# Weights decoded to half their value with a sign from ScalarE, and two heads gathered by matmul

## The chip, the cores and the metric

The kernel runs on one core of a Trainium2 chip. The metric is the device time of one execution in microseconds, median of the runs shown.

## The reference

Two stages follow each other: a linear attention with complex decay, and a feed-forward block. In short:

```python
# q, k, v, a_re, a_im: (4, 8, 768, 48); w_in (384, 2048), w_out (2048, 384)
mag = sqrt(a_re**2 + a_im**2); scale = minimum(mag, 0.999) / (mag + 1e-6)
a = (a_re + 1j * a_im) * scale
for t in range(768):                       # state S: (4, 8, 48, 48), complex
    S = a[:, :, t, :, None] * S + k[:, :, t, :, None] * v[:, :, t, None, :]
    y[:, :, t] = einsum("bhd,bhde->bhe", q[:, :, t], S.real)
x = y as (3072, 384)
h = x @ w_in;  g = h * sigmoid(1.702 * h);  out = g @ w_out
```

w_in and w_out are in double precision (the random factor times a float64 scalar), so the kernel is handed 64-bit words and makes single-precision numbers of them itself.

## The kernel before

**Tiling.** The 3072 tokens are 12 units of 256 (`T`). Unit 0 is prepared in two halves of 128 (`L`), the other units whole. Units form seven groups (`GROUPS`): unit 0, unit 1, then pairs. For each unit three things happen. `prepare` turns a_re, a_im, q and k into scaled and rotated q and k: squares, logarithms and exponentials on ScalarE, backward and forward products as scans on VectorE (`scan_sp`, L358, and `scan_qm`, L378), a running angle (L398), sine and cosine on ScalarE, then two rotations on VectorE (`rot0` into tile qr, `rot1` into tile qk). `remap` (L452 to L456) moves the rotated rows by DMA from a layout with 128 rows to one with 96 rows per head (tile qkh). `attend` computes scores, keys, outputs and state by small matmuls on TensorE. `moe` multiplies a group's outputs with w_in (`hidden`, L657), applies Silu on ScalarE, and multiplies with w_out (`project`, L686).

**Weights.** Eight blocks A0 to A7 of w_in and eight, U0 to U7, of w_out, each 128 x 768 64-bit words. `convert` decodes a block: a DMA loads it into one of four raw buffers; L249 shifts the top word left by three and masks it, L252 ORs in bits 31 and 30 of the top word, L255 (ScalarE) shifts the low word right by 29 in place, L256 adds. An integer add of tensors on VectorE runs as a custom operation on 16-bit halves. Group 0 uses the decoded single-precision values (`x`, `valA`, `valU`). From group 1 on each product is three products of rounded parts: `split` makes a high part by a ScalarE copy (L269) and a low part by a VectorE subtraction (L274); the matmuls then read `hiA`, `loA`, `xhi`, `xlo`.

**Checks of the input.** `inspect` and `angles` look over the data on VectorE; a slow general version stands behind a branch at the end and is not taken with this data.

**Order.** All operations are put into a plan with names of what they read and write, and issued in the order that the list `ORDER` (L1004) spells out. Each engine and the DMA queue of SyncE (SP) is in order, so `ORDER` sets each engine's queue. The durations in `add(...)` are the planner's; they set nothing at run time. ScalarE's table loads (L890) are put in where an operation's `tab` differs from the last one. Before the first scores there are 20 discarded matmuls against an identity (`WARM`, L434), 15 of them ahead of the first score matmul; they read the second rotation's tile.

**Set-up on POOL.** POOL makes the identity, the mask (12 small copies, L160), clears the two state tiles (L163), and then writes edge values (L338, L342, L392) that the scans read.

Of the kernel before, what the change touches and what calls it, by code (L numbers as in the profile page):

```python
# [8 lines left out]

# [4 lines left out]
U8 = mybir.dt.uint8  # L14
BF16 = mybir.dt.bfloat16
# [36 lines left out]
W_MIN = 2.0**-15  # L52
# [37 lines left out]
WARM = 20  # L90
# [5 lines left out]
def attention_moe(ctx: ExitStack, tc: tile.TileContext, qk_in, v, a_in, w_in, w_out, qn, kn, vn, an, bn, out):  # L96
# [65 lines left out]
    for x in st:  # L162
        nc.gpsimd.memset(x, 0.0)  # L163

# [19 lines left out]
    def d_t(n, fast=1.0):  # L184
        return 0.07 + n * 0.00104 / fast
# [47 lines left out]
    def convert(n):  # L233
# [6 lines left out]
        ulow = words.bitcast(U32)[:, :, 0]  # L240
        kg, kl = f"g{n % RAWS}", f"gl{n % RAWS}"
        rk = conv_rank(n)

        def ti():
            return weights.whole(m, j).bitcast(I32)
# [4 lines left out]
            out=ti(), in0=top, scalar1=3, scalar2=0x3FFFFFFF, op0=ALU.logical_shift_left, op1=ALU.bitwise_and,  # L250
        ), r=[kg], w=[f"v{c}"])
        add("DVE", d_t(WC), rk - 1, lambda: dve.scalar_tensor_tensor(  # L252
            out=ti(), in0=top, scalar=-(1 << 30), in1=ti(), op0=ALU.bitwise_and, op1=ALU.bitwise_or,
        ), r=[kg], w=[f"v{c}"])
        add("ACT", a_t(WC) - 0.1, rk - 1, lambda: act(out=low, in_=ulow, func=AF.Copy, scale=2.0**-29), w=[kl])  # L255
        add("DVE", d_t(WC), rk - 0.5, lambda: dve.tensor_tensor(out=ti(), in0=ti(), in1=low, op=ALU.add), r=[kl], w=[f"v{c}"])  # L256
# [41 lines left out]
    def prepare_part(u, i, a, b, np_, mag, den, rec, sp, th, *keys):  # L298
# [129 lines left out]
        for x, (dst, kd, fac, kf) in enumerate(((rv, "qr", cs, k_cs), (qv, "qk", t, k_th))):  # L428
# [3 lines left out]
            if u == i == 0 and x == 1:  # L432
                for k in range(WARM):
                    add("PE", 0.43, -WARM + k, lambda k=k, dst=dst: mm(  # L434
                        h_ps[0][:, k % 2 * T : (k % 2 + 1) * T], lhsT=ident, rhs=dst[:, k % NR, 0:T], start=True, stop=True
                    ), r=["qk0.0", "qk1.0"], w=["h0"])
# [3 lines left out]
            for some in ((0,), (1,)) if u == 0 else ((0, 1),):  # L440
                add("SP", REMAP * nn / (2 * T) * len(some) / 2, rk(f"rot{x}"), lambda dst=dst, x=x, some=some: remap(u, x, o, nn, dst, some),
                    r=ks(f"{kd}0", f"{kd}1") + ([f"last{x}"] if b == T else []), w=[f"H{hb_(u)}.{s}.{x}.{y}" for s in sub for y in some],
                    name=f"remap{u}.{i}.{x}" + ".1" * (some == (1,)), work=5)

# [180 lines left out]
    def moe(g):  # L625
# [7 lines left out]
        for order_, (lo, hi, f0) in enumerate(steps_):  # L633
# [30 lines left out]
            if whole:  # L664
                add("ACT", a_t(CW) - 0.15, rk(order_), lambda hb=hb, gb=gb: act(
                    out=high.g0(gb), in_=h_ps[hb], func=AF.Silu, scale=SLOPE
                ), r=[f"h{hb}"], w=[f"gh{gb}"], tab=SILU, name=f"G{u}.{order_}")
            else:
                add("ACT", a_t(CW) - 0.13, rk(order_), lambda hb=hb, gb=gb: act(out=high.g(gb), in_=h_ps[hb], func=AF.Silu, scale=SLOPE),  # L669
                    r=[f"h{hb}"], w=[f"gh{gb}"], tab=SILU, name=f"G{u}.{order_}")  # L670
                add("ACT", a_t(CW) - 0.13, rk(order_), lambda hb=hb: act(out=h_ps[hb], in_=h_ps[hb], func=AF.Silu, scale=SLOPE),  # L671
# [29 lines left out]
        for c in range(NR):  # L701
            buf, key = (osb[c], f"osb{c}")
            add("DVE", d_t(n_t), rk(len(steps_) + 0.1), lambda c=c, buf=buf: dve.tensor_scalar(
                out=buf[:, 0:n_t], in0=o_ps[c][:, 0:n_t], scalar1=1.0 / SLOPE, scalar2=None, op0=ALU.mult
# [442 lines left out]
```

## Time and profile before

| | us |
|---|---|
| median of 2 runs (552.05 to 552.52) | 552.28 |
| the profiled execution | 552.84 |
| its span, first to last instruction | 551.1 |
| TensorE matmul busy | 522.0 (95%) |
| VectorE busy | 390.0 (71%) |
| ScalarE busy | 362.2 (66%) |
| POOL busy | 11.9 (2%) |
| ScalarE table loads, 52 | 66.7 |

Engines in the profile: PE is TensorE's matmul, PEld its weight load, DVE is VectorE, ACT is ScalarE, SPq the DMA queue of SyncE. A single-precision matmul is two instructions in the trace. Busy shares are averages over stages that differ: the rows further down are cut by stage. Of a group of instructions, the mean is the duration of one; in a full queue the next one starts a little before the last one ends, so that the distance of two starts is shorter than the mean.

### The profile page before, as it was taken

To read this page: it belongs to the slowest core of one execution; us is meant where nothing else is said; L and a number is where in the kernel's file an instruction comes from. 1 tells how busy PE (TensorE), PEld (TensorE's weight loads), DVE (VectorE), ACT (ScalarE), POOL (GpSimd) and SP (SyncE) were. 2 spreads that over 40 slices of the span, in tenths; PEclk is the share of its full clock that TensorE was granted. 3 is DMA by queue.
4 is the path that set the end of the run, shared out by engine and by line. 5 is a ranking of instruction groups with operands and counts; after the bars stand their busy time and mean duration, and the time that the engine had idled before them with its cause. 6 is when DMAs were issued, how large, how long until landed. Compare 5 with 4: busy or idle time off the path is not lost.

```text
span 551.1 us, 14342 instructions
## 1 busy us (share of the span) xinstructions
PE 522.0 (95%) x6122; PEld 447.1 (81%) x6122; DVE 390.0 (71%) x625; ACT 362.2 (66%) x555; POOL 11.9 (2%) x55
## 2 busy tenths in 40 slices
PE   0399999999999999999999999999999999999997
PEld 0289988999988888888888888888888888888885
DVE  7999999999978787697598876785375524432232
ACT  7897899989699957968959578676425132232231
POOL 6000000000000000000000000000000000000000
PEclk9999999999999999999999999999999999999999
DMA  8867881835574764636548756518322552003101
GB/s 338 289 209 288 214 336 43 218 105 133 201 177 135 170 216 95 177 117 143 178 135 198 226 148 180 161 62 198 94 66 78 149 112 79 19 29 104 47 23 61
DMA packets 29253, 82.02 MB, mean 149 GB/s; under 512 B 4096, under 2 KB 7168, under 8 KB 29184
## 3 DMA queue, kind: packets, MB, share of 16 engines
q1 hardware_dynamic: 29184, 81.06, 50.6%
q8 instruction: 49, 0.80, 0.6%
q14 instruction: 20, 0.16, 0.1%
HBM read 57.41 MB, written 4.72 MB: 113 GB/s over the span
## 4 chain that ended last, share of the span: by engine, by line
PE 52%; ACT 2%; DVE 1%; issue 0%
PE o_ps L686 22%; PE h_ps L657 21%; PE x_ps L507 3%; PE z_ps L561 1%; PE z_ps L517 1%; PE p_ps L517 1%; PE p_ps L536 1%; PE z_ps L536 1%; ACT L890 0%; DVE qr L231 0%; ACT gh L669 0%; ACT h_ps L671 0%; ACT s L331 0%; ACT s L333 0%; ACT s L335 0%
## 5 line engine op out<-in xcount | busy, mean ns | idle before, releaser
L669 ACT ACTIVATE gh<-h_ps 128x512 fp32r<-128x512 f32 x88 | 52.1, 596 | 117.9 <-PE h_ps L657 92.2
L657 PE MATMUL h_ps<-xhi,hiA 128*128 128x512 f32 (+1 forms) x288 | 109.2, 379 | 0.0
L657 PE MATMUL h_ps<-xhi,loA 128*128 128x512 f32 (+1 forms) x288 | 107.1, 372 | 0.0
L657 PE MATMUL h_ps<-xlo,hiA 128*128 128x512 f32 (+1 forms) x288 | 107.1, 372 | 0.0
L673 DVE TENSOR_TENSOR gl<-h_ps,gh 128x512 fp32r<-128x512 f32 x88 | 60.0, 684 | 64.5 <-ACT h_ps L671 62.2
L686 PE MATMUL o_ps<-gh,hiU 128*128 128x512 f32 (+1 forms) x288 | 79.4, 376 | 0.2 <-ACT gh L669 0.2
L686 PE MATMUL o_ps<-gl,hiU 128*128 128x512 f32 (+1 forms) x288 | 79.6, 377 | 0.0
L686 PE MATMUL o_ps<-gh,loU 128*128 128x512 f32 (+1 forms) x288 | 78.1, 372 | 0.0
L890 ACT ACT_TABLE_LOAD x52 | 66.7, 1283 | 1.7 <-PEq L1135 0.9
L657 PEld LDWEIGHTS h_ps<-xhi,hiA 128*128 128x128 f32 x288 | 54.2, 188 | 10.9 <-DVE gl L673 1.2
L657 PEld LDWEIGHTS h_ps<-xhi,loA 128*128 128x128 f32 x288 | 54.3, 188 | 9.6
L657 PEld LDWEIGHTS h_ps<-xlo,hiA 128*128 128x128 f32 x288 | 54.3, 189 | 9.0
L686 PEld LDWEIGHTS o_ps<-gh,hiU 128*128 128x128 f32 x288 | 51.8, 188 | 10.4 <-ACT gh L669 0.7
L686 PEld LDWEIGHTS o_ps<-gh,loU 128*128 128x128 f32 x288 | 52.2, 188 | 9.5
L686 PEld LDWEIGHTS o_ps<-gl,hiU 128*128 128x128 f32 x288 | 51.2, 188 | 9.0 <-DVE gl L673 0.4
L671 ACT ACTIVATE h_ps<-h_ps 128x512 f32<-128x512 f32 x88 | 51.9, 594 | 0.0
L231 DVE TENSOR_TENSOR qk<-qk,s 128x768 f32<-128x768 f32 (+2 forms) x39 | 43.9, 1134 | 0.2
L723 DVE TENSOR_REDUCE fit<-raw_w 128x1 f32<-128x384 f32 x64 | 33.4, 544 | 14.4 <-DMA raw_w<-in_w_out_dram 12.8
L507 PE MATMUL x_ps<-pm,v 128*32 128x128 f32 x768 | 38.7, 274 | 0.0
L507 PE MATMUL x_ps<-qkh,st 96*32 96x128 f32 x640 | 33.7, 272 | 0.0
L434 PE MATMUL h_ps<-qk,ident 128*128 128x256 f32 x40 | 12.0, 458 | 22.7 <-DVE qk L231 22.7
L577 DVE TENSOR_TENSOR st<-z_ps,st 96x384 f32<-96x384 f32 x16 | 8.8, 552 | 28.2 <-PE z_ps L561 28.2
(104 smaller groups left out, 789.3 us busy)
## 6 DMA issues: line engine op xcount, KB each, us to landing
v<-in_v_dram SPq DMA_DIRECT2D x24, 416.0 KB, 4.5
ri<-in_a_dram SPq DMA_DIRECT2D x11, 768.0 KB, 6.5
qk<-in_qk_dram SPq DMA_DIRECT2D x11, 768.0 KB, 6.9
qkh<-qr SPq DMA_DIRECT2D x22, 288.6 KB, 5.9
qkh<-qk SPq DMA_DIRECT2D x22, 288.6 KB, 5.4
raw<-in_w_in_dram SPq DMA_DIRECT2D x8, 768.0 KB, 5.4
raw<-in_w_out_dram SPq DMA_DIRECT2D x8, 768.0 KB, 5.5
raw_w<-in_w_in_dram SPq DMA_DIRECT2D x16, 384.0 KB, 3.4
```

What stands on the lines that cost most here:

```text
L231: add(en, t, rank, lambda: e.tensor_tensor(out=out, in0=a, in1=b, op=alu), **kw)
L434: add("PE", 0.43, -WARM + k, lambda k=k, dst=dst: mm(h_ps[0][:, k % 2 * T : (k % 2 + 1) * T], lhsT=ident, rhs=dst[:, k % NR, 0:T], start=T ...
L507: mm(x_ps[32 * j : 32 * j + 32, r, :], lhsT=lt, rhs=rt, start=n == 0, stop=n == len(steps) - 1)
L517: mm(ps_[to : to + QL, j, lo:L], lhsT=at(h, 1, c)[:, lo : lo + QL], rhs=at(h, 0, c)[:, lo:L], start=True, stop=True)
L536: nc.tensor.transpose(banks[h // 4][0][:, h % 4, 0:KD], at(h, 1, c), ident[0:KD, 0:KD])
L657: mm(h_ps[hb][:, k * n_x : (k + 1) * n_x], lhsT=ww[:, r * T + f * P : r * T + (f + 1) * P], rhs=x[:, r, xs], start=n == 0, stop=n == last)
L669: add("ACT", a_t(CW) - 0.13, rk(order_), lambda hb=hb, gb=gb: act(out=high.g(gb), in_=h_ps[hb], func=AF.Silu, scale=SLOPE), r=[f"h{hb}"], ...
L671: add("ACT", a_t(CW) - 0.13, rk(order_), lambda hb=hb: act(out=h_ps[hb], in_=h_ps[hb], func=AF.Silu, scale=SLOPE), w=[f"h{hb}"], tab=SILU, ...
L673: add("DVE", d_t(CW), rk(order_), lambda hb=hb, gb=gb: dve.tensor_tensor(out=glo[gb], in0=h_ps[hb], in1=high.g(gb).bitcast(F32), op=ALU.su ...
L686: mm(o_ps[c][:, xs], lhsT=y[:, f * DM + c * P : f * DM + (c + 1) * P], rhs=x[:, k * n_x : (k + 1) * n_x], start=begins and k == 0 and n == ...
L723: add("DVE", d_t(CK), rk + 2, lambda x=x, op=op: dve.tensor_reduce(out=f_w[:, x, n : n + 1], in_=weights.looked_at()[:, :, 1], op=op, axis ...
L890: nc.scalar.preload_act_table_set(o[5])
```

## The change

- **Decoding.** The mask of the shift and the OR go. A new ScalarE activation, Sign, replaces the top word in place by +1.0 or -1.0 in single precision. The add takes as one operand the lower half of the low word and the upper half of that 1.0 (halves 0 and 3 of each group of four), which adds the sign bit and 127 to the exponent field. The result is half of the weight. Silu's scale is doubled, and the last multiplication is by 2/1.702, to make up for it; the lower limit for weights is doubled.
- **Heads 6 and 7 of unit 0, first half.** The six remap DMAs of these heads go. `gather` brings their rows to the 96-row layout by eight matmuls with columns of an identity (`pick`, made by two POOL copies in unused rows of a state tile) into tile h_ps1, and one ScalarE copy moves them to qkh.
- **Warm-up.** 14 pairs of 128-column matmuls instead of 20 matmuls of 256 columns; they read the tile that the first backward scan writes, and 11 of them stand ahead of the gather, 3 behind it.
- **ORDER** is a new list: among other things the DMA queue starts with the two pieces of a for unit 0, then A2, U0, A1 and the two pieces of q and k, and the first half of unit 0 runs ahead of most decodings.

```diff
-        add("DVE", d_t(WC, 2), rk - 1, lambda: dve.tensor_scalar(
-            out=ti(), in0=top, scalar1=3, scalar2=0x3FFFFFFF, op0=ALU.logical_shift_left, op1=ALU.bitwise_and,
-        ), r=[kg], w=[f"v{c}"])
-        add("DVE", d_t(WC), rk - 1, lambda: dve.scalar_tensor_tensor(
-            out=ti(), in0=top, scalar=-(1 << 30), in1=ti(), op0=ALU.bitwise_and, op1=ALU.bitwise_or,
-        ), r=[kg], w=[f"v{c}"])
+        limbs = raw.bitcast(U16).rearrange("p (n w) -> p n w", w=4)[:, :, 0:4:3]
+        add("DVE", d_t(WC, 2), rk - 1, lambda: dve.tensor_scalar(
+            out=ti(), in0=top, scalar1=3, scalar2=None, op0=ALU.logical_shift_left,
+        ), r=[kg], w=[f"v{c}"])
         add("ACT", a_t(WC) - 0.1, rk - 1, lambda: act(out=low, in_=ulow, func=AF.Copy, scale=2.0**-29), w=[kl])
-        add("DVE", d_t(WC), rk - 0.5, lambda: dve.tensor_tensor(out=ti(), in0=ti(), in1=low, op=ALU.add), r=[kl], w=[f"v{c}"])
+        add("ACT", a_t(WC) - 0.1, rk - 1, lambda: act(out=words[:, :, 1], in_=top, func=AF.Sign), w=[kg])
+        add("DVE", d_t(WC), rk - 0.5, lambda: dve._custom_dve(
+            ADD32_U16LIMBS, out=ti().bitcast(U16), in0=limbs, in1=ti().bitcast(U16), imm2=16,
+        ), r=[kl, kg], w=[f"v{c}"])
...
+    pick = st[1][2 * D : P]
+    nc.gpsimd.tensor_copy(out=pick[:, KD - QL // 2 : KD + QL // 2], in_=ident[2 * D : P, 2 * D : P])
+    nc.gpsimd.tensor_copy(out=pick[:, 2 * KD : 2 * KD + QL // 2], in_=ident[2 * D : P, P - QL // 2 : P])
...
-            if u == i == 0 and x == 1:
+            if u == i == x == 0:
+                ready = w(sp, 1, 1)
                 for k in range(WARM):
-                    add("PE", 0.43, -WARM + k, lambda k=k, dst=dst: mm(
-                        h_ps[0][:, k % 2 * T : (k % 2 + 1) * T], lhsT=ident, rhs=dst[:, k % NR, 0:T], start=True, stop=True
-                    ), r=["qk0.0", "qk1.0"], w=["h0"])
+                    add("PE", 0.45, -WARM + k, lambda k=k, ready=ready: [mm(
+                        h_ps[0][:, j * P : (j + 1) * P], lhsT=ident, rhs=ready[:, (k + j) % NR, :], start=True, stop=True
+                    ) for j in range(2)], r=k_sp, w=["h0"])
...
-            for some in ((0,), (1,)) if u == 0 else ((0, 1),):
+            for some in ((0,),) if u == i == 0 else ((0,), (1,)) if u == 0 else ((0, 1),):
...
+            if u == i == 0:
+                add("PE", 1.8, rk(f"rot{x}"), lambda dst=dst, x=x: gather(x, dst), r=ks(f"{kd}0", f"{kd}1"), w=["h1"])
+        if u == i == 0:
+            add("ACT", 0.6, rk("rot1"), lambda: act(
+                out=qkh[hb_(0)][0:KD, H * o + 2 * NR * nn : H * (o + nn)], in_=h_ps[1][0:KD, :], func=AF.Copy
+            ), r=["h1"], w=[f"H{hb_(0)}.{s}.{x}.1" for s in sub for x in range(2)])
+
+    def gather(x, src):
+        for y in range(2):
+            for k, (r, at_) in enumerate(((2 * y, KD - QL // 2), (1, (KD - QL // 2, 2 * KD)[y]))):
+                lo = at_ - D * x - QL * k
+                mm(h_ps[1][0 : (D if x == 0 and k == 1 else KD), y * T : (y + 1) * T], lhsT=pick[:, lo : lo + (D if x == 0 and k == 1 else KD)],
+                   rhs=src[2 * D : P, r, 0:T], start=x == y == k == 0, stop=x == y == k == 1)
...
-                    out=high.g0(gb), in_=h_ps[hb], func=AF.Silu, scale=SLOPE
+                    out=high.g0(gb), in_=h_ps[hb], func=AF.Silu, scale=2 * SLOPE
...
-                out=buf[:, 0:n_t], in0=o_ps[c][:, 0:n_t], scalar1=1.0 / SLOPE, scalar2=None, op0=ALU.mult
+                out=buf[:, 0:n_t], in0=o_ps[c][:, 0:n_t], scalar1=2.0 / SLOPE, scalar2=None, op0=ALU.mult
...
 ORDER = """
+80 132 15 10 5 100 154 186 81 0 82 170 84 83 134 133 86 85 16 87 135 136 94 88
...
```

The numbers in ORDER are places in the plan: 0 to 79 are the 16 decodings, five operations each; from 80 on stands the first half of unit 0 (80 its load, 96 the backward scan, 111 the first rotation), 112 to 125 are the warm-up, 127 and 130 the gathers, 128 the second rotation, 131 the copy, 132 the second half's load.

## Rows read from the trace of the kernel before

**Rows 1.** Busy per stretch: us, then PE, PEld, DVE, ACT, POOL busy (instructions), clock, DMA.
```profile
0.00:22.55 22.55, 0.00 (x0) 0.00 (x0) 18.67 (x42) 17.89 (x34) 9.56 (x30) 1.00 0.86 332
22.55:31.71 9.16, 9.05 (x31) 7.33 (x31) 9.16 (x17) 8.10 (x11) 0.00 (x0) 1.00 0.73 220
31.71:97.07 65.36, 64.11 (x1004) 58.30 (x1003) 63.51 (x87) 58.82 (x85) 0.44 (x5) 1.00 0.68 218
97.07:145.00 47.93, 47.86 (x819) 46.70 (x818) 47.33 (x69) 43.30 (x64) 0.48 (x4) 1.00 0.63 173
145.00:546.93 401.93, 400.83 (x4276) 334.72 (x4274) 250.54 (x413) 234.07 (x364) 1.42 (x16) 1.00 0.45 122
```

**Rows 2.** TensorE in time: start us, duration, line, operation, out and in, shape, count.
```profile
22.66 9.12 PE L434 MATMUL h_ps<-qk,ident 128*128 128x256 f32 x30 [22.66 <-DVE qk L231]
31.71 0.76 PE L517 MATMUL p_ps<-qkh 96*32 96x128 f32 x32
...
97.07 0.47 PE L657 MATMUL h_ps<-xhi,hiA 128*128 128x256 f32 x1
```

**Rows 3.** Busy per stretch again, up to M and in the front.
```profile
0.00:97.07 97.07, 73.17 (x1033) 65.63 (x1033) 91.33 (x143) 84.81 (x129) 10.00 (x35) 1.00 0.73 245
...
4.04:13.90 9.86, 0.00 (x0) 0.00 (x0) 8.59 (x14) 9.56 (x20) 6.31 (x17) 1.00 1.02 409
22.66:27.50 4.84, 4.84 (x12) 3.85 (x13) 4.84 (x11) 3.95 (x7) 0.00 (x0) 1.00 0.85 226
27.60:31.70 4.10, 4.10 (x20) 3.34 (x18) 4.10 (x6) 4.04 (x5) 0.00 (x0) 1.00 0.57 207
```

**Rows 4.** The front in time, all engines (columns as in rows 2; SPq issues DMAs).
```profile
3.63 6.13 POOL L160 COPY mask<-mask 32x128 bf16<-32x128 bf16 x12
...
4.04 0.94 ACT L207 ACTIVATE s<-ri 128x384 f32<-128x384 f32 x2 [1.87 <-DMA ri<-in_a_dram]
...
9.83 0.77 POOL L163 MEMSET st<- 128x448 f32 x1
...
13.79 2.00 DVE L358 TENSOR_TENSOR_SCAN s<-s,s 128x129 f32<-128x129 f32 x6
...
13.90 1.28 ACT L890 ACT_TABLE_LOAD   x1
...
16.42 0.96 DVE L398 TENSOR_TENSOR_SCAN s<-runs,s 128x387 f32<-128x387 uint8 x1
...
17.29 1.21 DVE L378 TENSOR_TENSOR_SCAN s<-s,small,s 128x128 f32<-128x128 f32 x3
...
21.52 1.26 SPq L452 DMA_DIRECT2D qkh<-qr  x2
...
21.59 0.96 DVE L231 TENSOR_TENSOR qk<-qk,s 128x768 f32<-128x768 f32 x1
```

**Rows 5.** Groups by line: operation, shapes, count, busy us, mean ns, idle before.
```profile
L255 ACT ACTIVATE raw<-raw 128x768 int32<-128x768 uint32 x16 | 14.3, 913 | 0.0
...
L256 DVE CUSTOM_DVE_ANT_0 valA<-raw,valA 128x1536 uint16<-128x1536 uint16 x8 | 7.6, 955 | 0.0
...
L252 DVE SCALAR_TENSOR_TENSOR valA<-raw,valA 128x768 int32<-128x768 int32 x8 | 7.6, 946 | 0.0
...
L269 ACT ACTIVATE hiA<-valA 128x768 fp32r<-128x768 f32 x8 | 6.7, 833 | 0.4 <-DVE valU L256 0.4
```

**Rows 6.** VectorE in time: two adds, and a 1536-element pass with its successor.
```profile
84.03 0.94 DVE L256 CUSTOM_DVE_ANT_0 valA<-raw,valA 128x1536 uint16<-128x1536 uint16 x1
84.89 0.94 DVE L256 CUSTOM_DVE_ANT_0 valU<-raw,valU 128x1536 uint16<-128x1536 uint16 x1
...
90.90 1.75 DVE L231 TENSOR_TENSOR qr<-qk,s 128x1536 f32<-128x1536 f32 x1
92.57 1.05 DVE L256 CUSTOM_DVE_ANT_0 valU<-raw,valU 128x1536 uint16<-128x1536 uint16 x1
```

**Rows 7.** A remap DMA issued at 24.9 us: engine, count, KB, us to landing.
```profile
qkh<-qk SPq DMA_DIRECT2D x1, 144.0 KB, 3.0
```

More of the change, by code (lines that the diff above doesn't have):

```diff
@@ L8 @@
 from concourse._compat import with_exitstack
+from concourse.dve_ops import ADD32_U16LIMBS
 F32 = mybir.dt.float32
@@ L14 @@
 U8 = mybir.dt.uint8
+U16 = mybir.dt.uint16
 BF16 = mybir.dt.bfloat16
@@ L51 @@
 RAWS = len(RAW_IN)
-W_MIN = 2.0**-15
+W_MIN = 2.0**-14
 W_MAX = 2.0**17
@@ L87, in order @@
         return order
-WARM = 20
+WARM = 14
 REMAP = 4.0
@@ L665, in moe @@
                 add("ACT", a_t(CW) - 0.15, rk(order_), lambda hb=hb, gb=gb: act(
-                    out=high.g0(gb), in_=h_ps[hb], func=AF.Silu, scale=SLOPE
+                    out=high.g0(gb), in_=h_ps[hb], func=AF.Silu, scale=2 * SLOPE
                 ), r=[f"h{hb}"], w=[f"gh{gb}"], tab=SILU, name=f"G{u}.{order_}")
             else:
-                add("ACT", a_t(CW) - 0.13, rk(order_), lambda hb=hb, gb=gb: act(out=high.g(gb), in_=h_ps[hb], func=AF.Silu, scale=SLOPE),
+                add("ACT", a_t(CW) - 0.13, rk(order_), lambda hb=hb, gb=gb: act(out=high.g(gb), in_=h_ps[hb], func=AF.Silu, scale=2 * SLOPE),
                     r=[f"h{hb}"], w=[f"gh{gb}"], tab=SILU, name=f"G{u}.{order_}")
-                add("ACT", a_t(CW) - 0.13, rk(order_), lambda hb=hb: act(out=h_ps[hb], in_=h_ps[hb], func=AF.Silu, scale=SLOPE),
+                add("ACT", a_t(CW) - 0.13, rk(order_), lambda hb=hb: act(out=h_ps[hb], in_=h_ps[hb], func=AF.Silu, scale=2 * SLOPE),
                     w=[f"h{hb}"], tab=SILU, name=f"G{u}.{order_}")
```

145 rows, old and new, of the table ORDER are left out of this document.

## The prediction

> **What bounds the kernel now.** Look first at the stages: one table of busy time per stretch [rows 1]. From 31.71 us on TensorE has no gap to speak of: 64.11 of 65.36 us, then 47.86 of 47.93, then 400.83 of 401.93. Up to there it does nothing useful; its matmuls from 22.66 to 31.7 multiply an identity and are thrown away, and the first score matmul follows them without a gap [rows 2]. So the time is the moment at which real work begins, plus about 510 us of it, plus stalls. A reader would stop here and call TensorE the bound. The same table says more: VectorE is busy 9.16 of 9.16 us, 63.51 of 65.36 and 47.33 of 47.93 up to 145 us, and only then falls to 62%. Both engines are full at once in that stretch, so TensorE can't simply begin earlier: VectorE's results would have to come earlier too.
>
> The point at which to read this is the first split product of the second group, hiA times xhi, at 97.07 us [rows 2]; I call it M. In VectorE's queue all 16 weight decodings stand ahead of it. VectorE was busy 91.33 us up to M and idle 5.74 [rows 3]; 3.88 of that idle time lies before 22.55 [rows 1], where the second rotation of the first half unit ends [rows 4]. ScalarE was busy 84.81 up to M [rows 3]. After M TensorE waits for 1.2 us in all [rows 1]: what M loses, the end loses.
>
> **The change, part by part.**
>
> *The OR goes.* 16 scalar-tensor-tensor passes of 0.946 us [rows 5]; in a full queue one costs its spacing, 0.87 (the adds of the same 0.95 us follow one another at 0.86 [rows 6]). 16 x 0.87 = 13.9 us less on VectorE, all ahead of M. The shift keeps its size.
>
> *The sign comes.* 16 activations over the same strided words as the low-word copy, 0.913 us [rows 5], about 0.82 each when they follow one another: 13.1 us more on ScalarE, all ahead of M. No table load is added by the function itself if it is in every set as Abs and Copy are here; the new order has one load fewer ahead of M. Six activations of 768 columns, five of them copies to the high halves (0.83 [rows 5], 0.75 spaced), move behind M: 4.5 less; a new copy of 512 columns adds 0.6. ScalarE's work up to M: 84.8 + 13.1 - 4.5 + 0.6 - 1.3 = 92.7.
>
> *The add changes its operand.* Before, both operands of the add are whole 32-bit words seen as pairs of 16-bit halves: 128x1536 halves take 0.955 us [rows 5], the time of a 768-word pass (0.946, the OR). So its time goes by words, one per step. After, in0 takes the low half of one word and the high half of the next: its two halves are 6 bytes apart and no longer in one word. No row shows such an operand. Bounds: 0.87 spacing (the same add, pairs kept) and 1.67 (a two-operand pass over 1536 separate elements: 90.90 to 92.57 us [rows 6]). I take 1.67, because by number of separately addressed places that row is the nearer. 16 x 0.80 = 12.8 us more on VectorE.
>
> The Trainium skill, "VectorE: DVE Perf Modes", section "What auto-detection actually checks", says that the two-per-cycle mode for two sources needs every tensor 16-bit with step of plus or minus one; in0 has step 3. By that rule the add runs at one half per step and the sum below stands; by the row of the old add alone the sum would be the first rival. No run here shows it yet.
>
> *Three splits move ahead of M* (the subtractions of the low halves, 768-element passes of two operands like the OR, 0.87 spaced): +2.6. VectorE up to M: -13.9 + 12.8 + 2.6 = +1.5 us.
>
> *The front is reordered.* The first half unit's decay factors load first and its operations run ahead of the decodings. Walk to its second rotation, which ended at 22.55: ScalarE starts at 4.04 [rows 4] when the first piece lands; 17 activations of 384 columns at 0.48 (9.56 busy over 20 [rows 3]) end near 12.0. The backward scan waits for edge values that POOL writes after the memset that ends at 10.6 [rows 4]; the two new copies of identity columns stand between, at most 0.5 each (12 mask copies in 6.13), so 11.5. Half of six scans, 1.0: 12.5. A small state copy now stands ahead of the table load: 12.8, load 1.28 [rows 4], arctangent 0.5: 14.6. VectorE meanwhile does 0.55 + 0.33 + 0.4 and the forward scans (1.21 [rows 4]) to 15.0, the angle scan 0.96 to 15.9, the second half's backward scan 1.0, then small passes (0.5 each) to 19.2, the second half's angle scan to 20.1, first rotation 0.93 to 21.0, a shift and the second half's forward scans to 22.7; ScalarE's sine waits behind the sign of U0, which waits for that shift: 22.9. Second rotation 0.96 [rows 4]: 23.9, that is 1.3 later than before. Ahead of it VectorE does 2.6 us less than before (out: one shift, three ORs, two adds, 5.1 us; in: one shift, an angle scan, three scans, 2.5). So it idles 1.3 + 2.6 = 3.9 us more in the front. In the kernel before, decodings filled that hole.
>
> *Heads 6 and 7 by matmul.* SP issues 4 remap DMAs instead of 10 (0.63 us each [rows 4]). Added: 16 matmul instructions of 256 columns, 0.21 each (20 in 4.10 us [rows 3]), 3.4 us on an otherwise empty TensorE, and a ScalarE copy that stands behind the second half's sine. First scores: 23.9 + 1.26 for two issues + 3.0 to land [rows 4, 7] = 28.2, against 31.71: 3.5 us earlier. It is worth nothing if VectorE reaches M late. Second scores wait for the copy, near 28.7.
>
> *Warm-up.* The discarded matmuls now start at about 12.6 and leave gaps of 1 to 2.5 us until the scores. In the trace the first 12 take 4.84 us and the next 20 take 4.10 [rows 3], 1.2 against 2.4 GHz by their spacing, though the clock column prints 1.00 in both. If the clock fell in a gap, about 2.5 us of TensorE time would go, hidden here by its wait for VectorE, and on the path if VectorE were not the bound.
>
> *Scales (2 x SLOPE, 2/SLOPE) and limits* change constants only: nothing.
>
> **Sum.** M comes 1.5 + 3.9 = 5.4 us later; later idle time of VectorE (1.85 from 31.71 to M [rows 1]) could shrink by up to 0.9. The new order has 0.7 us less real TensorE work ahead of M, so 0.7 more behind it. End: +5.2 to +6.1, less 0.4 for small differences between equal passes: about +5. The profiled execution took 552.84 us with a span of 551.1, and 0.56 more than the median of 552.28; the shift is applied to the median: 557.
>
> **Rivals.**
>
> 1. *The add keeps its pair rate.* For it: the same program, same count, 0.955 us in the trace. Then VectorE reaches M at 102.5 - 12.8 = 89.7 and ScalarE is the bound: 92.7 of work plus 4.4 idle in the walk above, plus 0.5 to 2 later: 97.6 to 99.1, against 97.07 and with the 0.7 of work behind M +1.2 to +2.7; with 1.5 us less idle than in the walk, -0.3. 552 to 555, about 553.5.
>
> 2. *Not slower: the front's gain survives.* TensorE starts at 28.2 and stalls as before, 2.4 us in all: 3.5 + 2.9 us (the discarded matmuls between its first operations) earlier, 546. M would then lie at 90.7. It needs the pair rate, and it decides when ScalarE's work up to M, with the 4 us before its first activation, falls under that: 6 us less than I count. Against it is the load in [rows 3]. With half of it, 546 to 551.
>
> 3. *Slower: the two queues take turns.* Each decoding now goes VectorE, ScalarE, VectorE: the add waits, at the head of VectorE's in-order queue, for a sign that stands behind other activations and table loads; behind that add wait the scans and rotations of the next unit, for which SP's remaps and TensorE's scores wait. Price: one sign (0.8) per decoding, 16 x 0.8 = 12.8 us beyond the forecast, at worst 570. It decides when ScalarE lags VectorE at the adds; in my walk ScalarE has some 5 us in hand at M, and in the new order most signs stand well ahead of their adds.
>
> **How the numbers follow.** Within 2% (541.2 to 563.3) is about what a measurement of this kernel can tell from no change. Forecast 0.68: 554.5 to 560, the likeliest 557. Rival 1, 0.18. Rival 2, 0.07. Rival 3, 0.07, of which two thirds lie above 563.3. Leaving out half of rival 2 and most of rival 3 gives 550 to 562. Faster by over 2% needs 11 us, more than rival 2 can give: 0.01. Slower by over 2%: 0.05.
>
> **What would show it.** The add's mean (about 1.75 us if right, 0.96 if rival 1). No OR; 16 signs near 0.9 us. VectorE idle 7 to 8 us up to the second rotation near 24. M near 102; then VectorE's share up to M stays above 90%. First scores near 28 with TensorE stalls of some 10 us between them and M: if TensorE runs without stalls from 28 on, my bound is wrong. ScalarE waits on shifts, or VectorE on signs by more than 3 us in all, speak for rival 3. The forecast is wrong if M comes before 98.

## The result, and the profile after

The changed kernel takes 560.2 us in the median of two runs (559.39 and 561.02), against 552.28 us before. The ratio is 1.0136, with a 95% interval of 1.0102 to 1.017: some 1.4% slower, clear of 1 and inside the 2% that the prediction called no change. The profiled execution took 559.39 us, with a span of 557.7: 6.6 us more span than before.

Busy time per stretch in the changed kernel, columns as in [rows 1]; the last three lines go up to M (the first split product of the second group), from M to the end, and from the first scores to M:

```profile
0.00:22.55 22.55, 10.26 (x52) 8.52 (x52) 15.94 (x41) 18.61 (x36) 8.17 (x32) 1.00 0.77 295
22.55:31.71 9.16, 8.70 (x92) 7.01 (x92) 8.28 (x11) 8.23 (x13) 0.00 (x0) 0.63 0.56 167
31.71:97.07 65.36, 58.31 (x896) 52.65 (x896) 62.03 (x73) 57.77 (x84) 0.40 (x4) 0.95 0.71 234
97.07:145.00 47.93, 46.01 (x672) 43.95 (x675) 45.99 (x63) 46.13 (x66) 0.37 (x5) 1.00 0.53 141
...
0.00:102.98 102.98, 81.51 (x1060) 71.93 (x1061) 92.09 (x128) 90.47 (x139) 8.57 (x36) 0.93 0.72 238
...
102.98:557.70 454.72, 449.91 (x5096) 381.53 (x5094) 298.48 (x482) 287.07 (x438) 1.68 (x21) 1.00 0.45 126
...
28.00:102.98 74.98, 65.85 (x989) 59.38 (x989) 71.44 (x81) 67.10 (x95) 0.40 (x4) 0.94 0.72 226
```

In 31.71 to 97.07 TensorE has gaps of 7.05 us, where before it had 1.25 [rows 1]. From M to the end of the span it is 454.72 us, against 454.03 before (551.1 less 97.07): 0.69 us of the loss lies behind M, and 5.91 ahead of it. TensorE in time, answering to [rows 2]:

```profile
11.18 7.91 PE L441 MATMUL h_ps<-s,ident 128*128 128x128 f32 x44 [11.18 <-DVE s L364]
19.89 2.35 PE L464 MATMUL h_ps<-qr,st 32*96 32x256 f32 x8 [0.79 <-DVE qr L236]
22.60 2.61 PE L464 MATMUL h_ps<-qk,st 32*96 32x256 f32 x8 [0.36 <-DVE qk L236]
25.14 2.93 PE L441 MATMUL h_ps<-s,ident 128*128 128x128 f32 x12
28.00 1.30 PE L539 MATMUL p_ps<-qkh 96*32 96x128 f32 x32
...
98.75 4.58 PE L708 MATMUL o_ps<-g,valU 128*128 128x256 f32 x20 [1.68 <-ACT g L687]
102.98 0.47 PE L679 MATMUL h_ps<-xhi,hiA 128*128 128x256 f32 x1
```

The first scores come 3.71 us earlier than before, and M 5.91 us later. The decoding, answering to [rows 5] (sign L259, low bits L258, add L260, shift L255; the last column is what the engine waited for ahead of the group):

```profile
L259 ACT ACTIVATE raw<-raw 128x768 f32<-128x768 int32 x16 | 14.8, 923 | 7.4 <-DVE valU L255 7.2 <-DVE valA L255 0.2
...
L258 ACT ACTIVATE raw<-raw 128x768 int32<-128x768 uint32 x16 | 14.3, 910 | 0.0
L260 DVE CUSTOM_DVE_ANT_0 valA<-raw,valA 128x1536 uint16<-128x1536 uint16 x8 | 14.0, 1749 | 0.1
L260 DVE CUSTOM_DVE_ANT_0 valU<-raw,valU 128x1536 uint16<-128x1536 uint16 x8 | 14.0, 1748 | 1.1 <-ACT raw L259 1.1
...
L255 DVE TENSOR_SCALAR valA<-raw 128x768 int32<-128x768 int32 x8 | 4.5, 563 | 1.2 <-DMA raw<-in_w_in_dram 1.2
```

The OR is gone, 16 signs of 0.92 us have come, and the add has grown from 0.955 to 1.749 us. A decoding cost 0.56 + 0.95 + 0.95 us of VectorE and 0.91 of ScalarE; now it costs 2.31 and 1.83. It is 0.77 us dearer in sum. VectorE gains only 0.15 of it.

The chain of waits just ahead of M (start, us, what), in the changed kernel. VectorE waits for no other engine from 72.28 on; the sign of 95.25 that had waited for a shift stands in the second fence:

```profile
72.28 1.76 DVE valA L260
...
94.74 0.47 DVE valU L255
95.21 0.87 DVE loA L280
96.08 1.67 DVE qk L236
97.75 1.67 DVE valU L260
99.42 0.87 DVE s L236
100.29 0.88 DVE loA L280
...
101.19 0.97 DVE loU L280
...
102.19 0.96 DVE loA L280
103.14 0.48 DVE xlo L593
...
103.67 0.39 PE h_ps L679
```

```profile
95.25 1.04 ACT L259 ACTIVATE raw<-raw 128x768 f32<-128x768 int32 x1 [2.03 <-DVE valU L255]
96.16 1.57 ACT L212 ACTIVATE s<-ri 128x768 f32<-128x768 f32 x2
97.63 1.07 ACT L687 ACTIVATE g<-h_ps 128x512 f32<-128x512 f32 x2
```

Two things end almost together at M. The 20 matmuls ahead of M in TensorE's queue begin at 98.75, when the activation g has come; the product just behind M waits for xlo, which VectorE has ready at 103.6 behind its last subtraction. As for g, it stands in ScalarE's queue behind a sign that could not overwrite its word until VectorE's shift had read it. Both paths lead back to VectorE's queue.

### The profile page after: what moved, and what is told of

It reads as the page before. It is cut to its first block, busy times and chain, and to the rows that moved or that the text cites. A ratio compares the mean times of both kernels' runs of the same rounds, so it can differ in the third digit from the quotient of the medians.

```text
span 557.7 us, 14412 instructions
## 1 busy us (share of the span) xinstructions
PE 531.4 (95%) x6154; PEld 453.5 (81%) x6154; DVE 390.6 (70%) x609; ACT 377.5 (68%) x575; POOL 10.2 (2%) x57
## 4 chain that ended last, share of the span: by engine, by line
PE 82%; DVE 11%; ACT 5%; DMA 1%; issue 1%; SPq 0%; ACTq 0%; DVEq 0%
PE o_ps L708 33%; PE h_ps L679 33%; PE x_ps L529 6%; PE z_ps L539 2%; PE p_ps L539 2%; PE z_ps L583 2%; DVE valU L260 2%; DVE valA L260 2%; DVE qk L236 1%; PE p_ps L558 1%; DVE s L364 1%; PE z_ps L558 1%; DVE s L384 1%; DMA raw<-in_w_out_dram 1%; ACT raw L259 1%
## 5 line engine op out<-in xcount | busy, mean ns | idle before, releaser
L708 PE MATMUL o_ps<-g,valU 128*128 128x128 f32 (+1 forms) x144 | 24.9, 327 | 5.7 <-ACT g L687 5.0
L708 PEld LDWEIGHTS o_ps<-g,valU 128*128 128x128 f32 x144 | 21.4, 204 | 7.5 <-ACT g L687 5.3
```

The lines of the kernel that those rows point to most:

```text
L708: mm(o_ps[c][:, xs], lhsT=y[:, f * DM + c * P : f * DM + (c + 1) * P], rhs=x[:, k * n_x : (k + 1) * n_x], start=begins and k == 0 and n == ...
```

## The experiments

M and the busy time up to M are from each profiled run; before 97.07 us (VectorE 91.33, ScalarE 84.81 [rows 3]), the changed kernel 102.98 (92.09, 90.47). Ratios are to the kernel before, run beside on the same chip, with 95% intervals. Its median was 551.95 to 553.68 us there, so an expected time, which counts from 552.28, is met or missed by up to 1.4 us through that alone: the ratio is the safer reading. The changed kernel was timed twice, the others 4 to 12 times.

| run | median us | ratio (interval) | M | VectorE, ScalarE busy up to M |
|---|---|---|---|---|
| changed | 560.2 | 1.0136 (1.0102-1.017) | 102.98 | 92.09, 90.47 |
| e1 add on whole words | 554.9 | 1.0046 (1.0023-1.0069) | 98.41 | 80.81, 90.09 |
| e2 16-bit sign | 564.73 | 1.0229 (1.0207-1.0251) | 109.00 | 81.57, 105.69 |
| e3 OR, new order | 563.07 | 1.0205 (1.0185-1.0225) | 103.90 | 92.71, 77.44 |
| e4 sign, old order | 562.25 | 1.0187 (1.0169-1.0204) | 105.28 | 89.59, 96.20 |
| e5 no warm-up | 561.15 | 1.0176 (1.0145-1.0207) | 103.07 | 92.07, 90.47 |
| e6 no low bits | 560.95 | 1.0163 (1.0129-1.0197) | 103.64 | 92.34, 78.72 |
| e7 e1 + e6 | 553.24 | 1.0019 (1.0006-1.0031) | 97.17 | 80.35, 78.52 |
| e8 sign on GpSimd | 570.82 | 1.0331 (1.0299-1.0364) | 114.74 | 89.02, 84.47 |
| e9 e7 + e5 | 555.3 | 1.0042 (1.0025-1.0058) | 96.22 | 80.23, 78.60 |
| e10 two passes, new order | 559.05 | 1.0099 (1.0083-1.0115) | 99.89 | 84.95, 77.56 |
| e11 two passes, old order | 554.25 | 1.0022 (1.0008-1.0036) | 98.86 | 84.81, 85.07 |
| e12 two splits back | 560.81 | 1.0131 (1.0112-1.0149) | 106.30 | not used |

From M to the end of the span ten of the twelve took 453.5 to 455.6 us (e9 456.1, e10 457.4), so M can be read as the result of a profiled run. That run is not always typical: its time was 1.9 us under the median in e3, 1.2 under it in e9, 0.6 above it in e7 and 2.2 above it in e12.

**e1: what does the add pay for?**

```diff
-        limbs = raw.bitcast(U16).rearrange("p (n w) -> p n w", w=4)[:, :, 0:4:3]
+        limbs = raw.bitcast(U16).rearrange("p (n w) -> p n w", w=4)[:, :, 2:4]
```

> The changed kernel with one thing different: the add reads the two halves of the upper word (the sign activation's whole 32-bit result), which lie side by side, and no longer one half of the lower and one half of the upper word, 6 bytes apart. The three lowest bits of the mantissa are left out by that. Queue, waits, instruction counts stay. If the distance of the halves is what the add pays for: add near 0.95 us instead of 1.75, VectorE about 12 us lighter up to M, M from 102.98 to 97-100 (ScalarE's queue ends last then), time 553-557. Rival, the custom add goes at its rate whatever the operand: add stays at 1.75, M 102-104, time 559-561. Second rival, the two queues' turns set M: add near 0.95, but M stays above 102.

The two groups of the add in e1:

```profile
L260 DVE CUSTOM_DVE_ANT_0 valU<-raw,valU 128x1536 uint16<-128x1536 uint16 x8 | 7.6, 955 | 1.4 <-ACT raw L259 1.4
...
L260 DVE CUSTOM_DVE_ANT_0 valA<-raw,valA 128x1536 uint16<-128x1536 uint16 x8 | 7.6, 950 | 0.4 <-ACT raw L259 0.3
```

Same program, same count of halves, nearly the same waits: 0.95 us instead of 1.75. The place of the two halves is the price; whether it is their distance, or that they lie in two words, e1 and e2 can't tell apart, since their halves are neighbours in one word. M falls by 4.57 us for 11.3 us less VectorE work, so something else ends last then. The first theory held in every number; that ScalarE's queue would be what ends last, e7 does not bear out. The words here still lie 8 bytes apart, and only the halves within a word are neighbours.

**e2: the same add, whole function.**

```diff
+        upper = raw.bitcast(BF16).rearrange("p (n w) -> p n w", w=4)[:, :, 1]
-        limbs = ...[:, :, 0:4:3]
+        limbs = ...[:, :, 0:2]
-        add("ACT", ..., lambda: act(out=words[:, :, 1], in_=top, func=AF.Sign), w=[kg])
+        add("ACT", ..., lambda: act(out=upper, in_=top, func=AF.Sign), r=[kg], w=[kl])
```

> The changed kernel, the sign written as a bfloat16 into the free upper half of the word that holds the low bits (behind the low-bit activation), so that the add finds both halves side by side; the whole function is kept. The sign no longer waits for the shift, since it doesn't write the word that the shift reads. If the distance of the halves is the cost: add near 0.95, M 97-100, time 553-557, and ScalarE's 7.2 us of waits of the sign on the shift gone. If the rate belongs to the custom add: add 1.75, M 101-104, time 558-561; if in that case the sign's waits also mattered, up to 2 us earlier.

The sign's group in e2:

```profile
L260 ACT ACTIVATE raw<-raw 128x768 bf16<-128x768 int32 x16 | 30.8, 1924 | 0.0
```

The add was 0.95 us, as expected, and no sign waited for a shift. But writing 16 bits into every fourth half takes ScalarE 1.92 us instead of 0.92. ScalarE is then busy 105.69 of 109.00 us and is the bound. The expected time was missed by nearly 8 us, for a cost that no row had shown.

**e3 and e4: the order alone, the decoding alone.** e3 is the changed kernel with the OR decoding of before put back (the scales with it); e4 is the kernel before with the new decoding:

```diff
 e4, in the decoding of the kernel before
-        add("DVE", d_t(WC), rk - 1, lambda: dve.scalar_tensor_tensor(
-            out=ti(), in0=top, scalar=-(1 << 30), in1=ti(), op0=ALU.bitwise_and, op1=ALU.bitwise_or,
+        add("ACT", a_t(WC) - 0.1, rk - 1, lambda: act(out=words[:, :, 1], in_=top, func=AF.Sign), w=[kg])
```

> The changed kernel's order, front, 0/1 matmuls and warm-up, with the decoding of before (OR on VectorE, no sign, add on whole words). Theory (VectorE's load and its front idle set M): VectorE has 13.9 us of OR back and loses 12.8 us of add, so M stays near 102-104 and the time near 558.5-560.5: the reordering alone makes most of the loss. Rival (the decoding and its turns of two queues make the loss): M 97-98.5, time 552-554.

> The order, front and copies of the kernel before, with only the decoding changed (sign on ScalarE in the OR's place in the order, add on halves 6 bytes apart, scales). VectorE is 1.1 us lighter, ScalarE 14.8 us heavier on 84.8 busy up to M at 97.07. Theory that VectorE alone sets M: M 95-98, time 551-554. Rival, ScalarE becomes the bound since this order has no room for 16 signs: M 100-106, time 556-562.

Busy time up to M, e3 and then e4:

```profile
0.00:103.90 103.90, 80.89 (x1061) 70.24 (x1061) 92.71 (x143) 77.44 (x122) 8.24 (x36) 0.93 0.69 231
```

```profile
0.00:105.28 105.28, 74.50 (x1032) 65.71 (x1032) 89.59 (x126) 96.20 (x144) 8.24 (x35) 1.00 0.69 226
```

In e3 M fits VectorE's load, 0.9 us after the changed kernel's with 0.6 us more work; the median is 2.6 us above the range expected. In e4 VectorE has less to do and M is 8.2 us late (2.4 of it already at the first scores, 34.15): ScalarE, busy 96.20 of 105.28 us, is the fuller engine there, so the rival holds. By the medians each alone costs more (2.05% and 1.87%) than both together (1.36%), though e4's interval touches that of the changed kernel. The parts don't add up; that each list of order fits the loads of its own decoding is my reading, which no run tests further.

**e5: does the clock's fall cost anything?**

```diff
-                    ) for j in range(2)], r=k_sp, w=["h0"])
+                    ) for j in range(0)], r=k_sp, w=["h0"])
```

> The changed kernel without the 14 groups of discarded matmuls (28 of them, in 11.18-28.07 us). The granted clock of the changed kernel fell to 0.50 in three stretches (about 23.4-30.4, 33.6-37.0, 58-61.6 us), 13.6 us in all, in which TensorE did at half speed what would have taken 6.8 us less. If that is hidden, as the prediction has it (VectorE and not TensorE sets M): M 102-104, time 558.5-561 whatever the clock does, even if the scores at 28.0 run at 1.00. Rival, the falls cost time: without them M at 99-101 and time 555.5-558.

The stretch of the first scores in e5; its changed-kernel counterpart stands above with a clock of 0.63:

```profile
22.55:31.71 9.16, 8.88 (x84) 5.70 (x82) 8.14 (x11) 8.08 (x13) 0.00 (x0) 1.00 0.59 186
```

In e5 the clock column prints 1.00 up to M, and M did not move (103.07). The time, 561.15, is just above the range expected, and the ratio's interval overlaps that of the changed kernel. But the column alone says too much, as it did in [rows 3], where one matmul takes 0.40 and then 0.21 us, both at 1.00. Score matmuls and g's in e5, then two of these groups in the changed kernel:

```profile
27.59 1.29 PE L539 MATMUL p_ps<-qkh 96*32 96x128 f32 x32
...
36.14 0.79 PE L539 MATMUL p_ps<-qkh 96*32 96x128 f32 x32
...
58.45 2.28 PE L708 MATMUL o_ps<-g,valU 128*128 128x128 f32 x18 [3.31 <-ACT g L687]
```

```profile
36.04 1.42 PE L539 MATMUL p_ps<-qkh 96*32 96x128 f32 x32
...
58.43 3.64 PE L708 MATMUL o_ps<-g,valU 128*128 128x128 f32 x18 [3.30 <-ACT g L687]
```

By their durations the first scores ran at the lower level in e5 too: 1.29 us for 32, against 1.30 in the changed kernel and 0.76 before [rows 2]. What e5 takes away is the later falls, 0.63 and 1.36 us in the two groups shown, and M did not come earlier. So the later falls were hidden, as the prediction had it. That the slow first scores cost nothing either, e5 does not test; for it speaks that in the changed kernel's trace VectorE waits nowhere for a matmul up to M, and ScalarE 0.6 us in all.

**e6, e7, e9: which engine holds M?** e6 leaves out the low-bit activation; e7 is e6 with e1's add; e9 is e7 without the discarded matmuls.

```diff
-        add("ACT", a_t(WC) - 0.1, rk - 1, lambda: act(out=low, in_=ulow, func=AF.Copy, scale=2.0**-29), w=[kl])
+        add("ACT", 0.0, rk - 1, lambda: None, w=[kl])
```

> The changed kernel without the low-bit activation (16 x 0.91 us of ScalarE; the add then reads the raw word's lowest half in its place, so the values' low bits are arbitrary). ScalarE has 14.6 us less ahead of M, VectorE the same slow add. If VectorE sets M in the changed kernel: M 100-103 (at most the 3 us that VectorE waited for ScalarE behind the front come back), time 556.5-560. Rival, ScalarE sets M as much as VectorE: M 95-98.5, time 551-555.

> Both at once: the add on the whole sign word (0.95 us) and no low-bit activation; the three lowest mantissa bits are left out. With the add alone cheaper M fell only from 102.98 to 98.41, for 12.7 us less on VectorE. Theory, ScalarE stood right behind VectorE: M now falls by much more than the two alone, to 89-93 (then TensorE's own work from 28 us on, some 62 us, ends last), time 545.5-549.5. Rival, something else (the front's waits, loads) holds M: M 95-98, time 551.5-555.

> The kernel with the cheap add on the whole sign word and without low-bit activation (three mantissa bits left out, M 97.17) now also without the discarded matmuls. In it VectorE and ScalarE are each busy only 80 of 97 us ahead of M, and the chain runs through TensorE's gather and first scores at a granted clock of 0.54. Theory, TensorE's own queue is the third bound right behind the two others (64 us of work from the first scores at 28.0 to M), and there the fall of the clock does cost: M 93-95, time 549.5-551.5. Rival, loads or the front hold M: M 96.5-97.5, time 552.5-554.

e6 up to M:

```profile
0.00:103.64 103.64, 82.54 (x1061) 72.36 (x1061) 92.34 (x128) 78.72 (x123) 9.07 (x36) 0.92 0.71 236
```

Nearly 12 us less on ScalarE bought nothing, while 11 us less on VectorE (e1) brought 4.6: VectorE sets M in the changed kernel. M and the time of e6 even lie above their ranges (100 to 103, 556.5 to 560), and the signs now wait 13.3 us for VectorE's shifts instead of 7.4. With the cheap add (e7) the same 12 us on ScalarE bring 1.2 us of M. My theory of ScalarE right behind, with M at 89 to 93, failed. In e7 the chain of waits goes through TensorE's gathers and first matmuls, then through SP's issues to a weight load. e9 tested TensorE's share: its first scores come 1.8 us earlier than in e7 (27.72 and 29.52), though at the lower level in both (1.30 us for 32), and M comes at 96.22, 0.95 earlier, between the two expected ranges. Its time is above both and did not improve on e7. From its first scores to M TensorE worked 64.99 us and stalled 3.51, most of it before 40 us:

```profile
27.72:96.22 68.50, 64.99 (x989) 58.78 (x989) 60.62 (x83) 58.70 (x84) 0.34 (x4) 1.00 0.78 244
27.72:40.00 12.28, 10.22 (x230) 9.05 (x230) 10.05 (x14) 12.02 (x17) 0.13 (x2) 1.00 0.58 168
```

ScalarE is full there (12.02 of 12.28 us). e9's first scores lead those of the kernel before by 3.99 us [rows 2]; 2.06 of that go as stalls before 40 us, 1.59 of them in one wait of TensorE for an activation. What holds M in e7 and e9 in the end (weight loads, ScalarE in that stretch, or TensorE's stalls together) these runs don't settle.

**e8: the sign on an idle engine** (on the kernel before; in e8, e10 and e11 the inspection admits weights under 2 only, as their decoding requires, and within a decoding some places in `ORDER` are exchanged, the low bits coming earlier).

```diff
-        add("DVE", d_t(WC), rk - 1, lambda: dve.scalar_tensor_tensor(... bitwise_and ... bitwise_or ...
+        add("POOL", p_t(WC), rk - 1, lambda: pool.tensor_scalar(
+            out=upper, in0=top, scalar1=0.0, scalar2=32768.0, op0=ALU.is_lt, op1=ALU.mult,
+        ), r=[kg], w=[kl])
```

> The order and front of the kernel before; the OR (16 x 0.95 us on VectorE) gives way to an instruction on GpSimd, which stood idle from 20 us on: it writes 0 or 0x8000 (the sign) as 16 bits into the free upper half of the word with the low bits, by compare and multiply; shift, low-bit activation and add as before, full values, the add on whole words. VectorE 15 us lighter up to M, ScalarE unchanged. If VectorE set M before and GpSimd keeps pace (16 instructions of perhaps 2 us): M from 97.07 to 91-95, time 546.5-550.5. Rival, GpSimd is late or gets in VectorE's way: adds wait for it, M 97 or later, time 552 or more.

```profile
L255 POOL TENSOR_SCALAR raw<-raw 128x768 uint16<-128x768 int32 x16 | 65.9, 4199 | 25.7 <-DVE qr L232 10.8 <-ACT raw L254 10.6 <-issue 3.9
...
L258 DVE CUSTOM_DVE_ANT_0 valU<-raw,valU 128x1536 uint16<-128x1536 uint16 x8 | 9.4, 1173 | 5.7 <-POOL raw L255 5.7
```

GpSimd needs 4.2 us for each, twice the 2 us that I had assumed without a row. The adds wait 10.9 us for it, and 5.7 more that the profile puts down to a small memset right behind the first of them in GpSimd's queue. VectorE's own adds become longer too (1.17 and 1.08 us instead of 0.96). The rival holds, and by far.

**e10 and e11: a lighter decoding.** Shift and OR of the low bits in one pass, and an AND with (upper word OR 0x3FFFFFFF) in a second; e10 on the changed kernel without discarded matmuls, e11 on the kernel before.

```diff
+        add("ACT", ..., lambda: act(out=low, in_=ulow, func=AF.Copy, scale=2.0**-29, bias=-0.5), w=[kl])
+        add("DVE", ..., lambda: dve.scalar_tensor_tensor(
+            out=ti(), in0=top, scalar=3, in1=low, op0=ALU.logical_shift_left, op1=ALU.bitwise_or), ...)
+        add("DVE", ..., lambda: dve.scalar_tensor_tensor(
+            out=ti(), in0=top, scalar=0x3FFFFFFF, in1=ti(), op0=ALU.bitwise_or, op1=ALU.bitwise_and), ...)
```

> The changed kernel's order, front and 0/1 matmuls, no discarded matmuls, and a third decoding in two VectorE passes of 0.95 us: the upper word shifted and OR-ed with the low bits, then AND-ed with (upper word OR 0x3FFFFFFF); low bits from ScalarE rounded down; full values for weights under 2, no sign activation. VectorE 6.5 us lighter ahead of M than in the changed kernel (1.90 instead of 2.31 a block), ScalarE 14.8 us. Theory, TensorE's queue from 28.0 on ends last or nearly: M 93-97, time 549.5-553.5. Rival, VectorE's front idle and waits for the low bits: M 98-101, time 554-557.

> The kernel before, with only the decoding replaced by the two-pass one (shift with OR of the low bits, AND with the upper word OR 0x3FFFFFFF). VectorE 16 x 0.56 = 9 us lighter, ScalarE as before. Theory, in the kernel before TensorE had 64.1 us of work in the 65.4 from the first scores at 31.71 to M, so M moves only as far as the first scores do (one to three shifts fewer ahead of them) plus at most the 1.3 of stalls: M 94-96.3, time 549-551.5. Rival, VectorE alone sets M: M 88-91, time 543-546. Second rival, the earlier place of the low bits holds up ScalarE in the front: M 97 or later, 552 or more.

e11 from its first scores to M, and the line that gives those scores' start:

```profile
33.43:98.86 65.43, 63.94 (x1004) 58.10 (x1003) 59.37 (x76) 59.72 (x86) 0.44 (x5) 1.00 0.70 224
```

```profile
33.43 0.76 PE L517 MATMUL p_ps<-qkh 96*32 96x128 f32 x32
```

VectorE has 6.5 us less to do up to M, and M comes 1.8 later, because the first scores come 1.7 later (33.43 instead of 31.71 [rows 2]): two of the front's passes wait 2.7 us for the low bits. From the scores to M it is 65.43 us, before it was 65.36. So in the kernel before TensorE stands right behind VectorE: a lighter VectorE alone buys no more than the earlier scores that it leads to. Of my theory the principle held; its numbers did not, since the second rival (the low bits in the front) moved the scores. e10 came out as its rival in M; its time is 2 us above that range (0.7 by its ratio), with TensorE waiting 1.32 us for xlo just behind M. Neither version beats the kernel before.

**e12: two splits back behind M.** In `ORDER`, 268 and 270 (the low halves of U0 and A2) go behind 362, the first split product.

```diff
-501 268 358 270 255 502 475 500 359 254 259 503 362 285
+501 358 255 502 475 500 359 254 259 503 362 268 270 285
```

> The changed kernel with two subtractions of low halves (third and fourth: U0 and A2) moved in the order from ahead of M to right behind it, where the kernel before has them. In the changed kernel's chain of waits VectorE works without a gap from 72.3 to M and these two passes (0.95 us, 0.87 spaced) are the last but one and the last but two in it. If the step is what the prediction takes it for: M 1.7 to 1.9 us earlier, 101.1-101.4, and the time 557.5-559.5; TensorE then waits behind M for the two only if they come too late. Rival, the transposed activations (xlo) or another pass sets M: M 102.5-103.2 and the time 559-561.

The ratio did not move (1.0131 against 1.0136), though the two intervals are too wide to shut out the theory's 1.7 to 1.9 us (0.3%). The trace speaks for the rival: xlo waited 1.12 us for ScalarE where the splits had stood, and M followed the start of g's 20 matmuls by 4.23 us, as it does in the changed kernel: g and the activations for xlo end as late as the splits did. M itself, 106.30, fits neither range. The profiled run was the longest of four (563.0; the others 560.37 to 560.85). There ScalarE waited for discarded matmuls, which read a buffer that it was to overwrite:

```profile
30.14 0.84 ACT L212 ACTIVATE s<-ri 128x768 f32<-128x768 f32 x1 [1.83 <-PE h_ps L441]
```

The first scores came at 29.97 in it. Its M is not compared with that of the changed kernel for that reason, where the same wait is 0.42 us. It is 1.19 us in e6, 1.86 in e1 and 2.33 in e7, whose first scores come at 28.78, 29.11 and 29.52; without the discarded matmuls (e5, e9, e10) they come at 27.59 to 27.92. So M of e1 and of e7 contains some of it too.

## Why the prediction was right

The forecast case came true in its mechanism: VectorE set M (e1, e6), and M came 5.9 us later, forecast 5.4. The median rose by 7.9 us, forecast 5, and lies 0.2 above that case's 560; the profiled executions differ by 6.55, and the other 1.4 is how far each lies from its median. The 0.4 us that the sum takes off for equal passes has no row behind it. The sum held better than its terms. Up to M, against before:

| step | predicted | measured |
|---|---|---|
| VectorE's work (OR, add, splits) | +1.5 | +0.76 (92.09 - 91.33) |
| VectorE idle up to 22.55 | +3.9 | +2.73 (6.61 - 3.88) |
| VectorE idle later | -0.9 to 0 | +2.43 (4.28 - 1.85) |
| M | +5.4 | +5.91 |
| behind M | +0.7 | +0.69 |

Busy and idle time of any engine add up to M, so the table shows where the terms went, and not that VectorE set M; e1 and e6 show that. In the kernel before it holds in one direction only: more work on VectorE moves M, but 6.5 us less did not (e11), since TensorE stands level.

**The add changes its operand** was the step that decided. I chose 1.67 us between the two bounds, and adds follow one another at 1.67:

```profile
58.96 1.75 DVE L260 CUSTOM_DVE_ANT_0 valA<-raw,valA 128x1536 uint16<-128x1536 uint16 x1
60.63 1.75 DVE L260 CUSTOM_DVE_ANT_0 valU<-raw,valU 128x1536 uint16<-128x1536 uint16 x1
```

Rival 1 is out, and e1 shows the reason to be the operand, as given. The rule that the prediction names, from the Trainium skill, "VectorE: DVE Perf Modes", section "What auto-detection actually checks", came out right here: 1.749 us with a step of 3, and 0.95 with neighbouring halves. Rival 1 priced that kernel at 553.5; e1 took 554.9 (1.0046), so even a cheap add would not have put the change ahead.

**Three splits move ahead of M**: there are four low-half subtractions up to M instead of two, so +1.7 and not +2.6. And e12 shows that they aren't the last word on M.

**The front is reordered**: the walk was 1.3 us too slow, 0.8 of it by the start of the backward scan. I had put the two identity copies ahead of the edge values in GpSimd's queue, at up to 0.5 us each; they stand behind them, and take 0.21 and 0.20. The backward scan starts at 10.70 instead of 11.5, on ScalarE's word and not on GpSimd's. The second rotation ends at 22.55, as before, not at 23.9:

```profile
10.70 1.06 DVE L364 TENSOR_TENSOR_SCAN s<-s,s 128x129 f32<-128x129 f32 x3 [1.34 <-ACT s L223]
...
12.04 1.28 ACT L912 ACT_TABLE_LOAD   x1
...
21.59 0.96 DVE L236 TENSOR_TENSOR qk<-qk,s 128x768 f32<-128x768 f32 x1 [0.23 <-ACT s L433]
```

**Later idle time** was the wrong sign. I let it shrink; it more than doubled. What I had not walked through is that the sign overwrites the word that the shift reads, so ScalarE's queue stops until VectorE has come to the shift: 7.4 us in all, nearly all of it in four waits of 0.9 to 2.5. Behind one of them, of 1.66 us ahead of the sign at 52.31, ScalarE's sine (L433) starts only at 55.56, and VectorE's longest wait behind the front is for it:

```profile
56.41 1.76 DVE L236 TENSOR_TENSOR qk<-qk,s 128x1536 f32<-128x1536 f32 x1 [1.93 <-ACT s L433]
```

No run takes these waits away alone, so that they are the cause of the idle time is read from the trace and not tested. That is rival 3's turn-taking, in the other direction than I priced it; VectorE itself waited only 1.1 us for signs. My own sign for rival 3 (over 3 us of ScalarE waiting on shifts) did show, and the loss (at most 2.4 us of VectorE's idle time) was a fifth of its price. Front and work came out 1.2 and 0.7 us smaller than forecast and this 2.4 larger, and so M was right within 0.5: that is luck, errors that cancelled.

**Heads 6 and 7 by matmul**: first scores at 28.00 (forecast 28.2), and the agreement is luck. The rotation ended 1.3 us earlier than in my walk, and its remaps land 2.6 us after they are issued, by about 26:

```profile
22.57 1.14 SPq L474 DMA_DIRECT2D qkh<-qk  x2
```

What the scores then stand behind is TensorE's own queue, the gathers and 12 discarded matmuls up to 28.0, which I had taken to be empty. From there come 9.13 us of stalls up to M (forecast some 10): worth nothing here, as said. **Behind M**: the 0.69 is 1.11 us more TensorE work (449.91 against 448.80) and 0.42 less waiting, where I had forecast work alone.

**Warm-up**: the clock fell, by far more than 2.5 us' worth; e5 shows the later falls hidden, for the slow first scores no run of this decoding tests it. The waits under e12 show that the discarded matmuls are not free in every run.

## What to carry to other kernels

Where two engines are both nearly full, price a moved operation by the sum over both: here each decoding cost 0.77 us more and the lighter engine gained 0.15. Before taking load off the engine that sets a milestone, measure how far behind the next one stands from the point where its real work begins (here TensorE: 64 us of work in 65): that distance, not the load removed, bounds what it can bring. An activation in place on a word that another engine must read first ties two in-order queues together, and what it holds up are the operations behind it.

## What the runs showed of the hardware that was not expected

- ScalarE writing 768 16-bit values at a spacing of 8 bytes takes 1.924 us, and 0.926 us for 32-bit values at the same spacing (e2, e1).
- GpSimd takes 4.2 us for a compare-and-multiply over 768 elements per partition, int32 to spaced 16-bit values. That is 4.4 to 7.5 times what VectorE's passes over the same words take (0.95 and 0.56 us). The Trainium skill, "GPSIMD Engine Reference", section "4.1 Engine selection", puts one-input elementwise work there at roughly line rate; this trace does not agree.
- VectorE's adds average 1.08 and 1.17 us instead of 0.96 in the kernel in which GpSimd's 16 instructions run beside them (e8).
- TensorE's granted clock fell to 0.50 (1.2 of 2.4 GHz) near 24 us in the changed kernel, after discarded matmuls and gathers from 11.18 on with gaps of 0.79 and 0.36 us.
- The clock column can print 1.00 while matmuls take the time of the lower level: in e5, without the discarded matmuls, it prints 1.00 up to M, and the first 32 score matmuls take 1.29 us, as long as at 0.50 in the changed kernel (1.30), against 0.76 before.
